# Retention followed by a tanh-shrink feed-forward on one core: down product interleaved with the up product, factored polynomial, retention and weight conversion moved into block 0

## The chip, the core and the metric

The kernel runs on one core of one Trainium2 chip. A core has five engines that run beside each other and wait for each other by semaphores: TensorE (PE in the profile; its weight loads are PEld), VectorE (DVE), ScalarE (ACT), GpSimd (POOL) and SyncE (SP, which here issues all DMAs). The metric is device microseconds of one execution, the median of several; lower is better.

## The reference, cut to what matters

```
# first part: q, k, v are [4, 8, 768, 64] float32
for t in range(S):                                   # S = 768 positions
    state = gamma[h] * state + outer(k[t], v[t])     # per batch and head, 64x64
    y[t]  = scale * (q[t] @ state)
x = y.transpose(0, 2, 1, 3).reshape(3072, 512)
# second part: w_in [512, 2048], w_out [2048, 512], both float64
h   = x @ w_in
out = (h - tanh(h)) @ w_out
```

[...] For small h the difference h - tanh(h) is made by a polynomial in u = h*h, for u of at least 0.5 by subtracting.

## The kernel before

**Tiling.** The 3072 rows of x are 24 chunks of 128 positions, and 6 blocks of 4 chunks (512 rows). Each of the 32 weight pieces is [128, 512]. `chunk(ci)` makes one chunk of the first part: POOL scales q and k by decays (L167), PE transposes both (L173, into the tile tp), ACT copies them out of PSUM (L176), PE makes k'v for the running state (L184), DVE updates the state in four half-height operations (L195, L197), PE makes the scores (L203), DVE masks them (L208, two operations), PE adds the part of the earlier state (L214) and of the scores (L218) into y, and ACT copies y into xT (L221).

**The second part.** For block n and column tile m (16 of each block), `up(n, m)` makes h = x w_in as four matmuls of 512 columns (L229; each shows as two records in the trace, so 768 records in all). ACT copies h to SBUF (L233) and makes u = h*h (L234) and tanh (L235). POOL makes the mask u >= 0.5 (L236) and h - tanh(h) (L237). DVE runs a Horner chain of five operations (L240), a sixth that multiplies by h (L244), and a predicated copy (L246) that ends the tile g. `down(n, j)` multiplies g of all 16 column tiles by w_out, 16 matmuls into one accumulator in PSUM (L252, two records each), ACT copies it out (L255), and SP writes it (L256).

**Weights.** `weights` loads one piece and converts it: one ACT operation (L129), six DVE operations (L124, L126, L128, L132, L134, L135) and three POOL operations (L130, L131, L137).

**What sets the order.** The kernel is written in a plain order: eight chunks with the 16 pieces of w_in between them, then block by block all 16 `up`, with one chunk of two blocks ahead after every fourth, and then the four `down`. A scheduler reorders it: each engine's queue is the scheduler's. Tiles of PSUM are held by tag: h has two banks, o one, tp two, s two, y one. Each engine then runs its own queue strictly in order.

```
    for n in range(NB):
        for m in range(NM):
            up(n, m)
            ...
        for j in range(BLK):
            down(n, j)
```

Of the kernel before, what the change touches and what calls it, by code (L numbers as in the profile page):

```python
# [10 lines left out]
I32 = mybir.dt.int32  # L11
# [9 lines left out]
G = [  # L21
    0.3333333270366726,
    -0.1333324237000098,
    0.05394671405955269,
    -0.02168005900277128,
    0.00808936284945116,
    -0.002039037268817698,
]
# [3 lines left out]
def kernel(  # L32
# [34 lines left out]
    stage = ctx.enter_context(tc.tile_pool(name="stage", bufs=4))  # L67
    inp = ctx.enter_context(tc.tile_pool(name="inp", bufs=3))
    mid = ctx.enter_context(tc.tile_pool(name="mid", bufs=2))
    xp = ctx.enter_context(tc.tile_pool(name="xp", bufs=3))  # L70
    tmp = ctx.enter_context(tc.tile_pool(name="tmp", bufs=2))
    gp = ctx.enter_context(tc.tile_pool(name="gp", bufs=20))
    op = ctx.enter_context(tc.tile_pool(name="op", bufs=2))
    ps = ctx.enter_context(tc.tile_pool(name="ps", bufs=1, space=bass.MemoryType.PSUM))

    def bank(tag, bufs):
        return ps.tile([P, TB], F32, tag=tag, name=tag, bufs=bufs)
# [5 lines left out]
    tab = cst.tile([P, tables.shape[1]], F32, name="tab")  # L83
    nc.sync.dma_start(out=tab, in_=tables)
    gq = tab[:, 0:H]
    gk = tab[:, H : 2 * H]
    gchunk = tab[:, 2 * H : 2 * H + NP]
    ident = tab[:, 2 * H + NP : 2 * H + NP + P]
    causal = tab[:, 2 * H + NP + P : 2 * H + NP + 2 * P]

    states = []
    for i in range(2):
        t = cst.tile([P, NP, P], F32, name=f"state{i}")
        nc.vector.memset(t, 0.0)
        states.append(t)

# [1 line left out]
    w1 = wts.tile([P, NC, DF], F32, name="w1")  # L98
    w2 = wts.tile([P, NM, DM], F32, name="w2")

    def work(tag, dtype=F32):
        return tmp.tile([P, TB], dtype, tag=tag, name=tag)

    def weights(dst, src):
# [10 lines left out]
        raw = stage.tile([P, 2 * TB], U32, tag="raw", name="raw")  # L115
        nc.sync.dma_start(out=raw, in_=src.bitcast(U32))
        raw = raw.rearrange("p (n two) -> p two n", two=2)
        lo, hi = raw[:, 0], raw[:, 1]
        head = work("h", U32)
        power = work("u", U32)  # L120
        low = work("th")
        e = work("a", U32)
        fits = work("m")
        nc.vector.tensor_scalar(head, hi, 3, 0x3FFFFFF8, op0=ALU.logical_shift_left,  # L124
# [4 lines left out]
        nc.scalar.activation(low, lo, AF.Copy, scale=2.0 ** -52)  # L129
        nc.gpsimd.tensor_tensor(low, low, power.bitcast(F32), op=ALU.mult)  # L130
        nc.gpsimd.tensor_tensor(dst, low, head.bitcast(F32), op=ALU.add)  # L131
        nc.vector.tensor_scalar(e, hi, 20, 0x7FF, op0=ALU.logical_shift_right,  # L132
                                op1=ALU.bitwise_and)
        nc.vector.tensor_scalar(fits, e, 1023.0 + 128.0, 3.0e38, op0=ALU.is_ge, op1=ALU.mult)  # L134
        nc.vector.scalar_tensor_tensor(fits, in0=e, scalar=1023.0 - 126.0, in1=fits,  # L135
                                       op0=ALU.is_ge, op1=ALU.max)
        nc.gpsimd.tensor_tensor(dst, dst, fits, op=ALU.mult)  # L137

    def load_w_in(fb):
        for c in range(NC):  # L140
            weights(w1[:, c, ts(fb, TB)], w_in[ts(c, P), ts(fb, TB)])

    def load_w_out(m):
        weights(w2[:, m], w_out[ts(m, P)])

# [1 line left out]
    loaded = {}  # L147
    xT = {}
    state = [None]
    n_state = [0]  # L150

    def load_chunk(ci):
        b, j = divmod(ci, CPB)
        loaded[ci] = []
        for nm, src in (("q", q), ("k", k), ("v", v)):
# [4 lines left out]
    def chunk(ci):  # L160
# [4 lines left out]
        qh, kh, vb = loaded.pop(ci)  # L165
        for t, g in ((qh, gq), (kh, gk)):
            nc.gpsimd.tensor_tensor(t, t, g[:, :, None].to_broadcast([P, H, D]), op=ALU.mult)  # L167

        turned = []
        for t in (qh, kh):  # L170
            tp = bank("tp", 2)
            for p in range(NP):
                nc.tensor.transpose(tp[:, ts(p, P)],  # L173
                                    t[:, ds(2 * p, 2)].rearrange("p h d -> p (h d)"), ident)
            s = mid.tile([P, NP, P], F32, tag=f"T{len(turned)}", name=f"T{len(turned)}_{ci}")
            nc.scalar.copy(out=s, in_=quarters(tp))  # L176
            turned.append(s)
        qT, kT = turned

        before = state[0] if j else None  # L180
        if j < CPB - 1:
            kv = bank("tp", 2)
            for p in range(NP):
                nc.tensor.matmul(kv[:, ts(p, P)],  # L184
                                 kh[:, ds(2 * p, 2)].rearrange("p h d -> p (h d)"),
                                 vb[:, ds(2 * p, 2)].rearrange("p h d -> p (h d)"),
                                 start=True, stop=True)
            after = states[n_state[0] % 2]
            n_state[0] += 1
            for i in range(2):  # L190
                r = ds(D * i, D)
                new, g = after[r, :, r], gchunk[r, :, None].to_broadcast([D, NP, D])
                src = quarters(kv)[r, :, r]
                if before is not None:
                    nc.vector.tensor_tensor(new, src, before[r, :, r], op=ALU.add)  # L195
                    src = new
                nc.vector.tensor_tensor(new, src, g, op=ALU.mult)  # L197
            state[0] = after

        sp = [bank("s", 2) for _ in range(2)]  # L200
        for h in range(H):
            r = ds(D * (h % 2), D)
            nc.tensor.matmul(sp[h % 2][:, ts(h // 2, P)], kT[r, h // 2], qT[r, h // 2],  # L203
                             start=True, stop=True)
# [129 lines left out]
```

## Time and profile before

| | |
|---|---|
| median of 3 runs | 1131.55 us (1128.22 to 1133.97) |
| span of the profiled execution (first to last instruction) | 1128.5 us; no time of its own is listed beside it |
| mean granted TensorE clock | 0.895 |
| PE busy | 885.3 us, 78% of the span |
| DVE busy | 794.2 us, 70% |
| POOL busy | 564.4 us, 50% |
| ACT busy | 242.9 us, 22% |
| moved by DMA | 42.63 MB, mean 38 GB/s |

The page cuts the span into 40 slices and gives each engine's busy share as a digit. Its chain is the work that ended last, followed back from the end; shares are of the span. Matmul records are pipelined: a record's duration is longer than the time from its start to the next one's start, so a rate is read from starts. A granted clock of 1.00 is 2.4 GHz and 0.50 is 1.2 GHz.

### The profile page before, as it was taken

Reading aid. Unit: us, or ns where it says so; the run is one execution under the profiler, and the core shown is the slowest. Engines: PE = TensorE matmul, PEld = TensorE weight load, DVE = VectorE, ACT = ScalarE, POOL = GpSimd, SP = SyncE. Lnnn points to the kernel's source line nnn. Section 1 sums busy time; section 2 is a strip of 40 time slices with the busy share of each in tenths; the row PEclk is TensorE's granted clock in tenths of the full one; section 3 lists DMA queues with packets and bytes.
Section 4 is the critical chain, followed back from the end, with each engine's and each line's share of the span. In section 5 each row is a group of like instructions: output and inputs, shape, how many; then the busy total and the mean of one; then the engine's idle time right before and its main releaser. Section 6 shows DMA issues by size and latency. Waiting matters only on the chain.

```text
span 1128.5 us, 8323 instructions
## 1 busy us (share of the span) xinstructions
PE 885.3 (78%) x2816; PEld 433.4 (38%) x2816; DVE 794.2 (70%) x986; ACT 242.9 (22%) x417; POOL 564.4 (50%) x340
## 2 busy tenths in 40 slices
PE   5336755657699987899777798888997788997788
PEld 4224521324244443444434343544443333433333
DVE  5999999899992599503999404999108996279910
ACT  2111221222231233102333002332003231132200
POOL 4877787766771357303555203565007872156800
PEclk9566967878899998899898899898999999998989
DMA  9344441211010001100111100000000000000000
GB/s 227 104 121 94 150 116 43 66 56 38 9 38 19 19 19 29 29 19 26 31 34 24 28 19 19 19 1 1 18 10 10 1 0 10 19 10 0 0 19 19
DMA packets 83131, 42.63 MB, mean 38 GB/s; under 512 B 75792, under 2 KB 75920, under 8 KB 83088
## 3 DMA queue, kind: packets, MB, share of 16 engines
q1 hardware_dynamic: 83088, 42.09, 14.2%
q8 instruction: 22, 0.36, 0.1%
q14 instruction: 21, 0.17, 0.0%
HBM read 35.79 MB, written 6.29 MB: 37 GB/s over the span
## 4 chain that ended last, share of the span: by engine, by line
DVE 52%; PE 32%; issue 10%; POOL 3%; ACT 2%; DMA 0%; ACTq 0%; SPq 0%; POOLq 0%; DVEq 0%
PE o L252 25%; DVE a L240 24%; DVE g L246 6%; DVE g L244 6%; PE h L229 4%; DVE a L132 3%; DVE h L124 3%; DVE a L208 2%; DVE m L134 2%; DVE state L197 2%; PE y L218 2%; POOL th L237 1%; DVE m L135 1%; DVE h L126 1%; DVE state L195 1%
## 5 line engine op out<-in xcount | busy, mean ns | idle before, releaser
L229 PE MATMUL h<-xT,w 128*128 128x512 f32 x768 | 395.5, 663 | 95.6 <-ACT h L233 95.6
L236 POOL TENSOR_SCALAR m<-u 128x512 int32<-128x512 f32 x96 | 218.9, 2281 | 416.2 <-ACT u L234 413.1
L252 PE MATMUL o<-w,g 128*128 128x512 f32 x768 | 349.8, 606 | 12.1 <-DVE g L246 9.9
L240 DVE SCALAR_TENSOR_TENSOR a<-a,u 128x512 f32<-128x512 f32 x384 | 344.4, 915 | 2.2
L229 PEld LDWEIGHTS h<-xT,w 128*128 128x128 f32 x768 | 156.4, 212 | 295.8 <-issue 177.1
L240 DVE SCALAR_TENSOR_TENSOR a<-u 128x512 f32<-128x512 f32 x96 | 85.8, 896 | 246.6 <-ACT u L234 246.5
L252 PEld LDWEIGHTS o<-w,g 128*128 128x128 f32 x768 | 144.6, 193 | 198.5 <-issue 162.7
L237 POOL TENSOR_TENSOR th<-h,th 128x512 f32<-128x512 f32 x96 | 143.8, 1498 | 20.4 <-ACT th L235 20.4
L233 ACT COPY h<-h 128x512 f32<-128x512 f32 x96 | 56.2, 585 | 364.9 <-DVE g L244 169.0
L246 DVE COPY_PREDICATED g<-m,th 128x512 f32<-128x512 int32 x96 | 86.6, 904 | 15.6 <-POOL th L237 14.8
L244 DVE SCALAR_TENSOR_TENSOR g<-a,h 128x512 f32<-128x512 f32 x96 | 85.2, 889 | 0.5
L218 PE MATMUL y<-a,v 128*64 128x128 f32 x384 | 45.4, 334 | 46.4 <-DVE a L208 46.3
L130 POOL TENSOR_TENSOR th<-th,u 128x512 f32<-128x512 f32 x32 | 53.0, 1656 | 45.9 <-DVE u L128 43.9
L255 ACT COPY o<-o 128x512 f32<-128x512 f32 x24 | 14.0, 585 | 281.2 <-PE o L252 281.1
L218 PEld LDWEIGHTS y<-a,v 128*64 128x64 f32 x384 | 31.9, 167 | 77.6 <-DVE a L208 66.6
L235 ACT ACTIVATE th<-h 128x512 f32<-128x512 f32 x96 | 60.0, 625 | 7.0 <-DVE g L246 7.0
L234 ACT ACTIVATE u<-h 128x512 f32<-128x512 f32 x96 | 60.6, 632 | 2.7
L173 PE MATMUL tp<-tab,q 128*128 128x128 f32 x96 | 17.1, 308 | 53.6 <-DVE state L195 38.1
L137 POOL TENSOR_TENSOR w<-w,m 128x512 f32<-128x512 f32 x32 | 49.0, 1531 | 11.6 <-DVE m L135 10.4
L203 PE MATMUL s<-T,T 64*128 64x128 f32 x384 | 38.6, 322 | 11.5 <-ACT T L176 11.4
L131 POOL TENSOR_TENSOR w<-th,h 128x512 f32<-128x512 f32 x32 | 42.6, 1333 | 2.3
L132 DVE TENSOR_SCALAR a<-raw 128x512 uint32<-128x512 uint32 x32 | 40.6, 1268 | 0.0
(28 smaller groups left out, 508.7 us busy)
## 6 DMA issues: line engine op xcount, KB each, us to landing
raw<-in_moe_w_in_dram SPq DMA_DIRECT2D x16, 512.0 KB, 4.2
raw<-in_moe_w_out_dram SPq DMA_DIRECT2D x16, 512.0 KB, 3.8
q<-in_q_dram SPq DMA_DIRECT2D x24, 256.0 KB, 3.4
k<-in_k_dram SPq DMA_DIRECT2D x24, 256.0 KB, 3.8
v<-in_v_dram SPq DMA_DIRECT2D x24, 256.0 KB, 3.1
out_dram<-o SPq DMA_DIRECT2D x24, 256.0 KB, 2.0
tab<-in_tables_dram SPq DMA_DIRECT2D x1, 138.0 KB, 2.3
```

Of the source, the lines that this page charges most:

```text
L132: nc.vector.tensor_scalar(e, hi, 20, 0x7FF, op0=ALU.logical_shift_right, op1=ALU.bitwise_and)
L218: nc.tensor.matmul(yT[ds(D * i, D), ts(p, P)], vb[:, h], a[i][:, p], start=(before is None and p == 0), stop=True, skip_group_check=True)
L229: nc.tensor.matmul(hp, w1[:, c, ts(m, P)], xT[n][:, c], start=(c == 0), stop=(c == NC - 1))
L233: nc.scalar.copy(out=h, in_=hp)
L234: nc.scalar.activation(u, h, AF.Square)
L235: nc.scalar.activation(th, h, AF.Tanh)
L236: nc.gpsimd.tensor_scalar(large, u, U_SMALL, None, op0=ALU.is_ge)
L237: nc.gpsimd.tensor_tensor(th, h, th, op=ALU.subtract)
L240: nc.vector.scalar_tensor_tensor(a, in0=prev, scalar=c / G[-1], in1=u, op0=ALU.add, op1=ALU.mult)
L244: nc.vector.scalar_tensor_tensor(g, in0=a, scalar=G[-1], in1=h, op0=ALU.mult, op1=ALU.mult)
L246: nc.vector.copy_predicated(g, large, th)
L252: nc.tensor.matmul(o_p, gT[n, m][:, ts(j, P)], w2[:, m], start=(m == 0), stop=(m == NM - 1))
```

## The change

**Order.** The automatic scheduler is off (`manual_schedule`): each engine's queue is in the order of the code. The first part's work of a chunk is cut into `load_chunk`, `scale_chunk`, `turn` (transposes and copies), `scores` (with the masks) and `outputs`. Eight chunks and eight weight pieces (four of w_in, four of w_out) come ahead of the second part; the other 16 chunks and 24 pieces stand inside block 0, one chunk with each column tile and two pieces with each of the first twelve. From block 1 on only `up`, `shrink` and `down` are left. The down product of a column tile follows the up product two tiles later (LAG), into four accumulators at once.

**Shrink.** ACT makes u, tanh, two squares (q0, q1) and the mask (a Relu of u - 0.5); all five read PSUM or u, and no copy of h is made. DVE makes two factors and their product (L270, L273, L274, L277), h - tanh(h) in place in PSUM (L272), and the predicated copy (L278), whose source is in PSUM. POOL has no part in it.

**Retention.** Decays are by position in the whole sequence, so the state needs no scaling; DVE updates it in one operation of 512 columns (L235 or L237). The state's part of y is eight products of 64 x 64 by 128 columns (L226) in place of four of 128 x 128.

**Conversion.** Two ACT operations (L145, L146), four DVE operations (L147, L149, L151, L153) and two POOL operations (L154, L155) for one piece.

**PSUM and SBUF.** All eight banks are one pool. The raw pieces have two buffers (four before), g five (twenty before), xT six.

```
+    AHEAD = 8
+    LAG = 2
...
+    ps = ctx.enter_context(tc.tile_pool(name="ps", bufs=8, space=bass.MemoryType.PSUM))
+    ctx.enter_context(tc.manual_schedule())
...
+    def convert(i):
...
+        nc.scalar.activation(low, lo, AF.Copy, scale=2.0 ** -52)
+        nc.scalar.activation(head.bitcast(F32), hi.bitcast(F32), AF.Abs)
+        nc.vector.tensor_scalar(head.bitcast(F32), head.bitcast(F32), HI_MIN, HI_MAX,
+                                op0=ALU.max, op1=ALU.min)
+        nc.vector.tensor_scalar(head, head, 3, 0x3FFFFFF8, op0=ALU.logical_shift_left,
                                 op1=ALU.bitwise_and)
         nc.vector.scalar_tensor_tensor(head, in0=hi, scalar=0xC0000000, in1=head,
                                        op0=ALU.bitwise_and, op1=ALU.bitwise_or)
         nc.vector.tensor_scalar(power, head, 0xFF800000, None, op0=ALU.bitwise_and)
         nc.gpsimd.tensor_tensor(low, low, power.bitcast(F32), op=ALU.mult)
         nc.gpsimd.tensor_tensor(dst, low, head.bitcast(F32), op=ALU.add)
...
+    def shrink(n, m):
+        hp = hps.pop((n, m))
+        u, th, q0, q1, large, t = (work(x) for x in ("u", "th", "q0", "q1", "large", "t"))
+        nc.scalar.activation(u, hp, AF.Square)
+        nc.scalar.activation(th, hp, AF.Tanh)
+        nc.scalar.activation(q0, u, AF.Square, bias=bias0)
+        nc.scalar.activation(q1, u, AF.Square, bias=bias1, scale=math.sqrt(A))
+        nc.scalar.activation(large, u, AF.Relu, bias=bias_m)
+        nc.vector.scalar_tensor_tensor(t, in0=u, scalar=R, in1=hp, op0=ALU.subtract,
+                                       op1=ALU.mult, reverse0=True)
+        nc.vector.tensor_tensor(hp, hp, th, op=ALU.subtract)
+        nc.vector.scalar_tensor_tensor(q0, in0=q0, scalar=C0, in1=t, op0=ALU.add, op1=ALU.mult)
+        nc.vector.scalar_tensor_tensor(q1, in0=q1, scalar=A * C1, in1=q0, op0=ALU.add,
+                                       op1=ALU.mult)
...
+        nc.vector.tensor_tensor(g, q1, u, op=ALU.mult)
+        nc.vector.copy_predicated(g, large.bitcast(I32), hp)
...
+    for ci in range(AHEAD):
+        scores(ci)
+        load_chunk(ci + 2)
+        scale_chunk(ci + 1)
+        if ci + 1 < AHEAD:
+            turn(ci + 1)
+        outputs(ci)
+        convert(ci)
+        load_weights(ci + 2)
...
     for n in range(NB):
         for m in range(NM):
+            ci = AHEAD + n * NM + m
+            if ci < NCH:
+                load_chunk(ci + 2)
+                convert(w)
+                load_weights(w + 2)
+                turn(ci)
             up(n, m)
+            if ci < NCH:
+                scores(ci)
+                scale_chunk(ci + 1)
+            shrink(n, m)
+            waiting.append((n, m))
+            downs(LAG)
+            if ci < NCH:
+                outputs(ci)
+                convert(w + 1)
+                load_weights(w + 3)
+                w += 2
```

The three places on which the prediction's terms rest follow. Names are tile, block and column tile (or chunk), and a buffer number. First PE from block 1 on; before, at the end of block 1 (o is an accumulator, g_1_14 the tile of column tile 14, h the next block's first product):

```order
L252 MATMUL o_2377<-w2_92,g_1_12_2246 128x512
L252 MATMUL o_2377<-w2_92,g_1_13_2269 128x512
L252 MATMUL o_2377<-w2_92,g_1_14_2292 128x512
L252 MATMUL o_2377<-w2_92,g_1_15_2315 128x512
L229 MATMUL h_2457<-xT_2_1064,w1_91 128x512
L252 MATMUL o_2397<-w2_92,g_1_0_1798 128x512
L252 MATMUL o_2397<-w2_92,g_1_1_1821 128x512
L252 MATMUL o_2397<-w2_92,g_1_2_1844 128x512
```

and now, inside block 1:

```order
L258 MATMUL h_1_5_2496<-xT_1_448,w1_89 128x512 x4
L284 MATMUL o_1_0_2434<-w2_90,g_1_3_2462 128x512
L284 MATMUL o_1_1_2436<-w2_90,g_1_3_2462 128x512
L284 MATMUL o_1_2_2438<-w2_90,g_1_3_2462 128x512
L284 MATMUL o_1_3_2440<-w2_90,g_1_3_2462 128x512
L258 MATMUL h_1_6_2523<-xT_1_448,w1_89 128x512 x4
L284 MATMUL o_1_0_2434<-w2_90,g_1_4_2489 128x512
L284 MATMUL o_1_1_2436<-w2_90,g_1_4_2489 128x512
L284 MATMUL o_1_2_2438<-w2_90,g_1_4_2489 128x512
L284 MATMUL o_1_3_2440<-w2_90,g_1_4_2489 128x512
```

The 16 matmuls into one accumulator have become four into four accumulators, for one g, behind the four of an up product two tiles later.

Second, POOL in the part ahead of the second part; before (q and k are chunk 3's, th, w1 and m belong to conversions):

```order
L130 TENSOR_TENSOR th_180<-th_180,u_179 128x512
L131 TENSOR_TENSOR w1_91<-th_180,h_178 128x512
L137 TENSOR_TENSOR w1_91<-w1_91,m_182 128x512
L167 TENSOR_TENSOR q_3_227<-q_3_227,tab_85 128x512
L130 TENSOR_TENSOR th_197<-th_197,u_196 128x512
L167 TENSOR_TENSOR k_3_229<-k_3_229,tab_85 128x512
L131 TENSOR_TENSOR w1_91<-th_197,h_195 128x512
L137 TENSOR_TENSOR w1_91<-w1_91,m_199 128x512
```

and now (low, w1 are conversions of pieces 2 and 3):

```order
L180 TENSOR_TENSOR k_3_204<-k_3_204,tab_87 128x512
L180 TENSOR_TENSOR q_3_206<-q_3_206,tab_87 128x512
L154 TENSOR_TENSOR low_2_327<-low_2_327,power_2_326 128x512
L155 TENSOR_TENSOR w1_89<-low_2_327,head_2_325 128x512
L180 TENSOR_TENSOR k_4_278<-k_4_278,tab_87 128x512
L180 TENSOR_TENSOR q_4_280<-q_4_280,tab_87 128x512
L154 TENSOR_TENSOR low_3_401<-low_3_401,power_3_400 128x512
L155 TENSOR_TENSOR w1_89<-low_3_401,head_3_399 128x512
```

The scaling of chunk ci + 2 now stands right behind the two operations of conversion ci, and a conversion has two operations in place of three.

Third, DVE in block 0; before (a, h, u, m of lines 124 to 135 belong to a conversion):

```order
L240 SCALAR_TENSOR_TENSOR a_946<-u_944 128x512
L124 TENSOR_SCALAR h_963<-raw_961 128x512
L240 SCALAR_TENSOR_TENSOR a_946<-a_946,u_944 128x512
L126 SCALAR_TENSOR_TENSOR h_963<-raw_961,h_963 128x512
L240 SCALAR_TENSOR_TENSOR a_946<-a_946,u_944 128x512
L128 TENSOR_SCALAR u_964<-h_963 128x512
L240 SCALAR_TENSOR_TENSOR a_946<-a_946,u_944 128x512
```

and now, one iteration (masks of chunk 16, shrink of column tile 8, state, then conversions 25 and 26 start):

```order
L209 TENSOR_TENSOR a0_16_1623<-s0_16_1613,tab_87 128x512
L209 TENSOR_TENSOR a1_16_1625<-s1_16_1614,tab_87 128x512
L270 SCALAR_TENSOR_TENSOR t_1634<-u_1629,h_0_8_1608 128x512
L272 TENSOR_TENSOR h_0_8_1608<-h_0_8_1608,th_1630 128x512
L273 SCALAR_TENSOR_TENSOR q0_1631<-q0_1631,t_1634 128x512
L274 SCALAR_TENSOR_TENSOR q1_1632<-q1_1632,q0_1631 128x512
L277 TENSOR_TENSOR g_0_8_1644<-q1_1632,u_1629 128x512
L278 COPY_PREDICATED g_0_8_1644<-large_1633,h_0_8_1608 128x512
L237 TENSOR_TENSOR state_16_1666<-kv_16_1661,state_15_1551 128x512
L147 TENSOR_SCALAR head_25_1677<-head_25_1677 128x512
L149 TENSOR_SCALAR head_25_1677<-head_25_1677 128x512
L151 SCALAR_TENSOR_TENSOR head_25_1677<-raw_25_1573,head_25_1677 128x512
L153 TENSOR_SCALAR power_25_1678<-head_25_1677 128x512
```

The conversions no longer alternate with the polynomial: the two masks, six operations of a shrink and the state's update stand together, and two whole conversions follow them. The shown rows end after the first.

## Rows read from the trace of the kernel before

**Rows 1.** The page: the span in 40 slices; the chain by engine.

```profile
span 1128.5 us, 8323 instructions
...
PE   5336755657699987899777798888997788997788
...
DVE  5999999899992599503999404999108996279910
...
DVE 52%; PE 32%; issue 10%; POOL 3%; ACT 2%; DMA 0%; ACTq 0%; SPq 0%; POOLq 0%; DVEq 0%
```

**Rows 2.** Groups by line: shapes xcount | busy us, mean ns | idle before.

```profile
L240 DVE SCALAR_TENSOR_TENSOR a<-a,u 128x512 f32<-128x512 f32 x384 | 344.4, 915 | 2.2
...
L208 DVE TENSOR_TENSOR a<-s,tab 128x512 f32<-128x512 f32 x48 | 31.7, 685 | 3.3 <-PE s L203 2.6
...
L129 ACT ACTIVATE th<-raw 128x512 f32<-128x512 uint32 x32 | 21.6, 676 | 74.1 <-POOL w L131 54.9 <-DVE g L246 17.6 <-DMA raw<-in_moe_w_in_dram 1.2
...
L221 ACT COPY xT<-y 128x512 f32<-128x512 f32 x24 | 14.0, 583 | 109.7 <-PE y L218 109.7
```

**Rows 3.** Timeline of PE, warm: start, us, operation, xrecords.

```profile
616.67 0.60 PE L173 MATMUL tp<-tab,q 128*128 128x128 f32 x4
617.11 0.60 PE L173 MATMUL tp<-tab,k 128*128 128x128 f32 x4
617.54 1.02 PE L252 MATMUL o<-w,g 128*128 128x512 f32 x2
618.40 1.05 PE L184 MATMUL tp<-v,k 128*128 128x128 f32 x8
619.39 1.16 PE L203 MATMUL s<-T,T 64*128 64x128 f32 x16
620.48 1.16 PE L214 MATMUL y<-T,state 128*128 128x128 f32 x8
```

**Rows 4.** Windows: length, busy us of PE, PEld, DVE, ACT, POOL; granted clock.

```profile
28.00:44.00 16.00, 8.21 (x38) 6.56 (x39) 16.00 (x16) 3.57 (x6) 13.56 (x10) 0.50 0.44 113
815.00:830.00 15.00, 15.00 (x36) 6.57 (x35) 0.00 (x0) 0.58 (x1) 0.00 (x0) 1.00 0.05 17
```

**Rows 5.** Timeline, first chunks.

```profile
4.69 1.04 POOL L167 TENSOR_TENSOR q<-q,tab 128x512 f32<-128x512 f32 x1 [4.27 <-DMA q<-in_q_dram]
...
6.88 1.11 PE L173 MATMUL tp<-tab,k 128*128 128x128 f32 x4
...
11.64 0.66 PE L173 MATMUL tp<-tab,q 128*128 128x128 f32 x4
...
13.44 1.09 PE L218 MATMUL y<-a,v 128*64 128x128 f32 x14
...
40.10 1.97 PE L218 MATMUL y<-a,v 128*64 128x128 f32 x14 [0.99 <-DVE a L208]
```

**Rows 6.** Timeline, conversions: DVE beside an idle and beside a busy POOL.

```profile
17.85 0.42 DVE L124 TENSOR_SCALAR h<-raw 128x512 uint32<-128x512 uint32 x1
...
18.52 0.68 DVE L126 SCALAR_TENSOR_TENSOR h<-raw,h 128x512 uint32<-128x512 uint32 x1
...
25.77 1.58 POOL L130 TENSOR_TENSOR th<-th,u 128x512 f32<-128x512 f32 x1 [1.37 <-DVE u L128]
26.15 1.48 DVE L124 TENSOR_SCALAR h<-raw 128x512 uint32<-128x512 uint32 x1
27.43 1.32 POOL L131 TENSOR_TENSOR w<-th,h 128x512 f32<-128x512 f32 x1
```

**Rows 7.** Timeline, second part: polynomial on DVE, an activation on ACT.

```profile
542.29 1.75 DVE L244 SCALAR_TENSOR_TENSOR g<-a,h 128x512 f32<-128x512 f32 x1
...
553.04 2.14 DVE L240 SCALAR_TENSOR_TENSOR a<-a,u 128x512 f32<-128x512 f32 x3
...
560.37 0.63 ACT L235 ACTIVATE th<-h 128x512 f32<-128x512 f32 x1
```

**Rows 8.** Timeline: the last copy out of PSUM.

```profile
1124.97 0.58 ACT L255 COPY o<-o 128x512 f32<-128x512 f32 x1 [14.13 <-PE o L252]
```

More of the change, by code (lines that the diff above doesn't have):

```diff
@@ L84, with columns, weight_ends, load_weights @@
     nc.sync.dma_start(out=tab, in_=tables)
[L85 to L95, printed above, removed]
+    at = [0]
+    def columns(n):
+        at[0] += n
+        return tab[:, at[0] - n : at[0]]
+    gq = columns(CPB * H)
+    gk = columns(CPB * H)
+    ident = columns(P)
+    causal = columns(P)
+    bias0, bias1, bias_m = columns(1), columns(1), columns(1)
     w1 = wts.tile([P, NC, DF], F32, name="w1")
     w2 = wts.tile([P, NM, DM], F32, name="w2")
-    def work(tag, dtype=F32):
-        return tmp.tile([P, TB], dtype, tag=tag, name=tag)
-    def weights(dst, src):
+    raws = {}
+    def weight_ends(i):
+        f, r = divmod(i, 2 * NC)
+        if r < NC:
+            return w1[:, r, ts(f, TB)], w_in[ts(r, P), ts(f, TB)]
+        m = NC * f + r - NC
+        return w2[:, m], w_out[ts(m, P)]
+    NW = 2 * NM
+    def load_weights(i):
+        if i >= NW:
+            return
+        dst, src = weight_ends(i)
         if src.dtype == F32:
@@ L178, in chunk @@
[L178 to L186, printed above, removed]
-                                 start=True, stop=True)
[L188 to L197, printed above, removed]
-            state[0] = after
@@ L200, in chunk @@
[L200 to L204, printed above, removed]
-        a = []
-        for i in range(2):
-            a.append(mid.tile([P, NP, P], F32, tag=f"a{i}", name=f"a{i}_{ci}"))
-            nc.vector.tensor_tensor(a[i], quarters(sp[i]),
-                                    causal[:, None, :].to_broadcast([P, NP, P]), op=ALU.mult)
@@ L211, in chunk @@
-        yT = bank("y", 1)
-        if before is not None:
-            for p in range(NP):
-                nc.tensor.matmul(yT[:, ts(p, P)], before[:, p], qT[:, p], start=(p == 0),
-                                 stop=False, skip_group_check=True)
+        kh, _, vb = loaded.pop(ci)
+        _, qT = turned.pop(ci)
+        a = masked.pop(ci)
+        before = state[0] if j else None
+        yT = bank(f"y_{ci}")
+        if before is not None:
+            for h in range(H):
+                r = ds(D * (h % 2), D)
+                nc.tensor.matmul(yT[r, ts(h // 2, P)], before[r, h // 2, r], qT[r, h // 2],
+                                 start=(h // 2 == 0), stop=False, skip_group_check=True)
@@ new lines, in outputs @@
+        if j < CPB - 1:
+            kv = bank(f"kv_{ci}")
+            for p in range(NP):
+                nc.tensor.matmul(kv[:, ts(p, P)], pair(kh, p), pair(vb, p),
+                                 start=True, stop=True)
+            after = mid.tile([P, NP, P], F32, tag="state", name=f"state_{ci}")
+            if before is None:
+                nc.vector.tensor_copy(after, quarters(kv))
+            else:
+                nc.vector.tensor_tensor(after, quarters(kv), before, op=ALU.add)
+            state[0] = after
@@ L224, with work @@
     gT = {}
+    o_p = {}
+    def work(tag, dtype=F32):
+        return tmp.tile([P, TB], dtype, tag=tag, name=tag)
+    hps = {}
     def up(n, m):
-        hp = bank("h", 2)
+        hp = bank(f"h_{n}_{m}")
         for c in range(NC):
@@ L259, in next_chunk, with down @@
-    def next_chunk(ci):
-        if ci + 2 < NCH:
-            load_chunk(ci + 2)
-        if ci < NCH:
-            chunk(ci)
+    def down(n, m, j):
+        if m == 0:
+            o_p[n, j] = bank(f"o_{n}_{j}")
+        nc.tensor.matmul(o_p[n, j], gT[n, m][:, ts(j, P)], w2[:, m], start=(m == 0),
+                         stop=(m == NM - 1))
+        if m == NM - 1:
+            o = op.tile([P, DM], F32, tag="o", name=f"o_{n}_{j}")
+            if j % 2:
+                nc.vector.tensor_copy(o, o_p[n, j])
+            else:
+                nc.scalar.copy(out=o, in_=o_p[n, j])
+            nc.sync.dma_start(out=out[ds(n * TB + j * P, P)], in_=o)
@@ L287, in _tables @@
+    for j in range(BLK):
+        for n, m in waiting:
+            down(n, m, j)
+def _tables(H, D, S=768):
     import numpy as np
```

167 lines of the change are left out of this document (78 added, 89 removed).

## The prediction

> **What bounds the kernel now.** I read the page's slices and chain first. In the slices PE and DVE take turns: from the middle of the span on, DVE stands at 9 for some slices while PE is at 7 or 8, and then DVE falls as low as 0 while PE is at 8 or 9 [rows 1]. The chain gives DVE 52% of the span and PE 32% [rows 1]. So a block is two phases one behind the other: 16 up products at the pace of DVE's polynomial, then four down products in which DVE has nothing to do. Then I looked for the pace of PE when nothing holds it. In a down phase it is busy all the time at a granted clock of 1.00, its upper level of 2.4 GHz [rows 4], and two records of 512 columns take 0.86 us from start to start, 0.43 each [rows 3]. A column tile has four up and four down products, 16 records: 6.88 us. For 96 tiles that is 660 us, far under the span. Last I looked at why DVE is slow where it is slow. Beside an idle POOL a one-input operation takes 0.42 us and a two-input one 0.68; beside a POOL product the same one-input operation takes 1.48 and ends only after the product [rows 6], and a two-input one 1.75 [rows 7]. The mean of the polynomial's operation is 0.915 [rows 2]. The mask from PSUM, which has one input in SBUF, stays at 0.685 on average [rows 2], so it doesn't wait for POOL.
>
> **The change, part by part.** I follow the new order in four stretches. Within a stretch I look for the loop that comes back to its own start; its length is the period.
>
> *Blocks 1 to 5.* PE's queue is four up products of tile m, four down products of tile m-2, and nothing else. PE needs 6.88 us a tile. DVE has six operations: two with an operand in PSUM at 0.685, and four in a dependent chain at 0.73 each (three such in 2.14 us with the last at 0.68 [rows 7]), 4.3 us. ACT has five at 0.63 [rows 7], 3.2 us. POOL has no instruction left, so nothing lengthens DVE's. g of tile m is ready some 5.5 us after its up product (two activations, 1.3, then DVE's 4.3), and its down product is due only after three more groups of 3.44 us on PE beyond the one that runs, 13.8 us. Hence PE doesn't wait; the two engines that are moved off the path hide beneath it, and would set the pace only above 6.88 us a tile. Waits for a bank stand only at column tiles 3 and 4 of a block, on copies of the last accumulators that have a whole group of 3.44 us to be made in. From the start of block 1 there are 80 tiles of up and 82 of down (two are behind): (80 + 82) x 8 = 1296 records x 0.43 = 557 us.
>
> *The last tile.* Its g is due 4.3 us after its up product (one group and one product) and ready after 5.5: 1.2 us of wait. From the last copy's start at 1124.97 to the span's end 3.5 us pass now [rows 1, 8], with the way from PE to the copy 3.8. Together 5.
>
> *Block 0, first twelve tiles.* Here PE has 6.88 us and a chunk: transposes 0.87, scores 1.09, k'v 0.99, the state's part as k'v 0.99, and y as the scores 1.09 [rows 3], 5.0 in all, so 11.9. The state's eight half-size products aren't in the trace; their bounds are half of that 0.99 and twice it. DVE has two conversions, two masks, the shrink and the state. PE's next up product waits for the state's update, since that releases its bank; so the loop runs through DVE. From the end of one update: the first conversion takes 3 x 0.42 + 0.68 + 3 hand-overs of 0.05 = 2.1. Now POOL starts on it, 1.66 from start to start and then 1.32 [rows 6], and DVE's second conversion runs into both products: two of its operations wait, and it ends at 6.6 in place of 4.2. The masks end at 7.9, the two operations on PSUM at 9.15. POOL meanwhile, from 6.7, does the second conversion's two products (3.0) and the scaling of two tiles (1.04 alone [rows 5], with DVE beside it 1.3), and is done at 12.3. Three two-input operations of the shrink get one slot behind each of POOL's last three: 12.7. The predicated copy makes it 13.4, the state 14.1. PE is done with k'v at 10 and does not set the loop. The period is 14.1 us, x 12 = 169. Bounds: if POOL and DVE never met, PE's 11.9 would hold (26 us less in all). If every DVE operation kept out of POOL's way, it would be DVE's 10.4 (two conversions 4.2, five operations on PSUM 3.3, four in the chain 2.9) and POOL's 2 x 3.0 + 2 x 1.3 = 8.6 in a row, 19.0 (59 us more).
>
> Two operations of the shrink, t and h - tanh(h), have one input in SBUF and one in PSUM. The row nearest to them is the mask's 0.685, the other end is the polynomial's 0.915 [rows 2]; I take the mask's. The Trainium skill (SBUF — State Buffer, Who interferes with whom) says that a DVE instruction with at most one SBUF input, outside its two-port modes, doesn't contend with GpSimd, and that with two it does; by it the period stays at 14.1. Were both held like the row of 1.48, it would be 15.7 and the total 19 us more.
>
> *Block 0, last four tiles.* No conversion is left: DVE's masks, shrink and state take 6.3, and PE's 11.9 hold. 4 x 11.9 = 48.
>
> *The eight chunks ahead.* This part gets a loop that the old order doesn't have. On PE, the transposes of chunk ci+2 stand ahead of the y of chunk ci+1; on POOL their scaling stands behind conversion ci; that one waits on ACT behind the copy of y of chunk ci. So from y to the next y everything stands in a row: copy and two activations 0.583 + 2 x 0.676 = 1.94 [rows 2], DVE's four operations 2.1, POOL's two products 3.0, two scalings 2.1, the last transposes 1.1, state, k'v and y, with 0.5 for five hand-overs between engines. PE waits over 6 us in it; in a stretch of the present kernel where PE is busy half the time its granted clock is 0.50, the lower level of 1.2 GHz [rows 4], and y takes 1.97 in place of 1.09 [rows 5]. All cold it is 16.5 us, all warm (transposes 0.6) 13.3. In the first chunk transposes are cold at 6.88 and warm at 11.64 [rows 5], so I take y alone as warm: 15.6. The first y ends at 14.5 [rows 5], six loops follow, 93.6, and from there to the end of chunk 8's transposes 10.6 (the loop without its last three terms and with 0.4 for hand-overs): the first up product starts at 118.7. DMA isn't in it: by the shapes a loop loads 1.25 MB, and each load is sent a loop ahead.
>
> *Sum.* 118.7 + 169 + 48 + 557 + 5 = 898 us of span. The runs' median is 3.05 above the profiled span; with it 901 us, 20% less than before.
>
> **The rivals.**
>
> *POOL and DVE exclude each other altogether in block 0.* For it: in the conversions of the present kernel nearly every one-input operation shows 1.48. Against it: the mask doesn't. 901 + 59 = 960.
>
> *The short loops.* PE stays warm in the first part and the two engines seldom meet: 901 - 6 x 2.3 - 26 = 861. Against it speaks the 0.50 [rows 4].
>
> *Slower: DVE sets blocks 1 to 5.* The tile in PSUM is read and written in place by DVE, and no row shows that, nor a predicated copy out of PSUM. If the six operations took as long as the longest row, 1.75 [rows 7], a tile would take 10.5 us: 901 + 80 x 3.62 = 1191. It turns slower than before above 1.63 us an operation, (1132 - 901) / 80 = 2.9 us more a tile. That row belongs to a busy POOL, and POOL's queue is empty there.
>
> *The overlap doesn't come about,* since something in PE's queue waits for g after all. A wait of 2.9 us a tile would bring the old time back; no instruction of PE's queue in those blocks waits on a tile younger than two.
>
> **How the numbers follow.** Forecast 0.70, POOL and DVE excluding each other 0.14, short loops 0.11, DVE sets the pace 0.04, no overlap 0.01. The predicted time is the first's, 901. The range goes from the short loops, 862, to 955, just under the first rival, which leaves out its upper half, the slower case and little else. A measurement of this kernel can tell 0.5%, some 6 us, from no change. Faster by more than that: 0.95; within: 0.01; slower: 0.04.
>
> **What would show it.** Blocks 1 to 5 right: PE without idle time at clock 1.00, 6.9 us from one h to the next, DVE near 60% and POOL at nothing. Block 0 right: some 14 us between state updates, DVE's one-input operations near 1.5 beside POOL. The first part right: 15 to 16 us from y to y, clock near 0.5, the first h near 119. Wrong: an h later than 140, idle time of PE that DVE ends in blocks 1 to 5, or any DVE operation over 1.1 us there.

## The result, and the profile after

The changed kernel takes 884.88 us (median of 5 runs, 880.28 to 886.51), where the kernel before takes 1131.55 (1128.22 to 1133.97): a ratio of 0.7818, with a 95% interval of 0.7794 to 0.7841. The prediction was 901 us, 862 to 955. The profiled execution took 880.28 us, with a span of 878.5; the median lies 6.4 us above that span. Of the four runs of the kernel with phases and two banks further down, one took 1132.91 us at a granted clock of 0.744, a slower state, and is left out of its median.

The page of the changed kernel, beside [rows 1]: the span, the slices of PE and DVE, the granted clock, and the chain's shares by engine.

```profile
span 878.5 us, 8488 instructions
...
PE   4644789898889999999999999999999999999997
...
DVE  2233499989996546555566555655556655566554
...
PEclk9778689999999999999999999999999999999999
...
PE 77%; DVE 13%; POOL 3%; issue 2%; ACT 2%; DMA 1%; SPq 0%; DVEq 0%; POOLq 0%; ACTq 0%
```

The turns of PE and DVE are gone. From the sixteenth slice to the last but one PE stands at 9 at full clock, DVE at 5 or 6 beside it. The chain, 52% DVE and 32% PE before, is 77% PE. DVE stands at 8 or 9 only in slices 6 to 12, which lie in the first twelve tiles of block 0.

The same by the prediction's stretches (ahead of the first h; twelve tiles of block 0; its last four; from block 1 to the last up product; the rest). The columns are busy time and instructions of each engine, the granted clock, the DMA share and rate.

```profile
core 0: us, PE busy (x) PEld busy (x) DVE busy (x) ACT busy (x) POOL busy (x), PEclk, DMA share, GB/s
0.00:105.17 105.17, 55.47 (x481) 45.17 (x481) 29.19 (x54) 25.39 (x44) 36.06 (x36) 0.79 0.55 121
105.17:268.95 163.78, 146.75 (x897) 85.60 (x897) 153.27 (x200) 78.92 (x142) 95.72 (x72) 0.95 0.55 134
268.95:316.82 47.87, 47.55 (x307) 27.49 (x305) 26.80 (x39) 18.56 (x33) 9.54 (x8) 1.00 0.16 31
316.82:862.40 545.58, 545.58 (x1274) 241.60 (x1273) 322.10 (x484) 235.92 (x406) 0.00 (x0) 1.00 0.03 10
862.40:878.50 16.10, 11.15 (x26) 4.47 (x24) 5.38 (x8) 4.08 (x7) 0.00 (x0) 1.00 0.17 65
```

In the fourth row PE is busy for all of its 545.58 us. One h follows the other by 6.87 us there, with a down group between them. Of the h that starts at 502.32, DVE's six operations run from 507.07 to 511.39, 4.32 us:

```profile
502.32 3.60 PE L258 MATMUL h<-xT,w 128*128 128x512 f32 x8
...
507.07 0.69 DVE L270 SCALAR_TENSOR_TENSOR t<-u,h 128x512 f32<-128x512 f32 x1 [2.55 <-ACT th L266]
...
509.19 3.60 PE L258 MATMUL h<-xT,w 128*128 128x512 f32 x8
...
510.66 0.73 DVE L278 COPY_PREDICATED g<-large,h 128x512 f32<-128x512 int32 x1
```

### The profile page after: what moved, and what is told of

The parts are those of the page before. It is cut to its first block, busy times and chain, and to the rows that moved or that the text cites. A ratio compares the mean times of both kernels' runs of the same rounds, so it can differ in the third digit from the quotient of the medians.

```text
span 878.5 us, 8488 instructions
## 1 busy us (share of the span) xinstructions
PE 806.5 (92%) x2976; PEld 404.3 (46%) x2976; DVE 536.7 (61%) x784; ACT 362.9 (41%) x629; POOL 141.3 (16%) x116
## 4 chain that ended last, share of the span: by engine, by line
PE 77%; DVE 13%; POOL 3%; issue 2%; ACT 2%; DMA 1%; SPq 0%; DVEq 0%; POOLq 0%; ACTq 0%
PE h L258 35%; PE o L284 34%; DVE head L151 2%; DVE head L149 2%; PE y L226 2%; PE y L241 2%; DVE q L274 1%; DVE g L277 1%; PE qTp L194 1%; PE kv L231 1%; DVE a L209 1%; DVE q L273 1%; PE kTp L194 1%; POOL low L154 1%; PE s L204 1%
## 5 line engine op out<-in xcount | busy, mean ns | idle before, releaser
L258 PE MATMUL h<-xT,w 128*128 128x512 f32 x768 | 351.3, 601 | 1.5 <-DVE g L278 1.5
L270 DVE SCALAR_TENSOR_TENSOR t<-u,h 128x512 f32<-128x512 f32 x96 | 65.7, 684 | 190.4 <-ACT th L266 190.4
L274 DVE SCALAR_TENSOR_TENSOR q<-q,q 128x512 f32<-128x512 f32 x96 | 74.9, 780 | 10.4 <-DVE q L273 0.5
L277 DVE TENSOR_TENSOR g<-q,u 128x512 f32<-128x512 f32 x96 | 73.8, 768 | 8.0 <-DVE q L274 0.5
L278 DVE COPY_PREDICATED g<-large,h 128x512 f32<-128x512 int32 x96 | 70.3, 732 | 9.9
L273 DVE SCALAR_TENSOR_TENSOR q<-q,t 128x512 f32<-128x512 f32 x96 | 70.5, 734 | 0.0
L267 ACT ACTIVATE q<-u,tab 128x512 f32<-128x512 f32 x96 | 69.3, 722 | 0.0
L268 ACT ACTIVATE q<-u,tab 128x512 f32<-128x512 f32 x96 | 68.9, 718 | 0.0
L269 ACT ACTIVATE large<-u,tab 128x512 f32<-128x512 f32 x96 | 68.7, 716 | 0.0
L272 DVE TENSOR_TENSOR h<-h,th 128x512 f32<-128x512 f32 x96 | 66.5, 692 | 0.0
L194 PE MATMUL kTp<-tab,k 128*128 128x128 f32 x96 | 20.3, 348 | 47.9 <-POOL k L180 47.9
L154 POOL TENSOR_TENSOR low<-low,power 128x512 f32<-128x512 f32 x32 | 41.2, 1287 | 130.3 <-DVE power L153 115.6
L244 ACT COPY xT<-y 128x512 f32<-128x512 f32 x24 | 14.1, 586 | 93.9 <-PE y L241 93.9
L155 POOL TENSOR_TENSOR w<-low,head 128x512 f32<-128x512 f32 x32 | 41.4, 1292 | 2.5
```

Source lines behind the costliest of these rows:

```text
L258: nc.tensor.matmul(hp, w1[:, c, ts(m, P)], xT[n][:, c], start=(c == 0), stop=(c == NC - 1))
L267: nc.scalar.activation(q0, u, AF.Square, bias=bias0)
L268: nc.scalar.activation(q1, u, AF.Square, bias=bias1, scale=math.sqrt(A))
L269: nc.scalar.activation(large, u, AF.Relu, bias=bias_m)
L270: nc.vector.scalar_tensor_tensor(t, in0=u, scalar=R, in1=hp, op0=ALU.subtract, op1=ALU.mult, reverse0=True)
L272: nc.vector.tensor_tensor(hp, hp, th, op=ALU.subtract)
```

## Experiments on the interleave

The theory: blocks 1 to 5 gain because ACT's and DVE's work of a tile lies wholly beside PE's 6.88 us, and two tiles of lag cover the way from h to g. The rival: the shorter polynomial and the empty POOL bring the gain, whatever the order.

**Phases again.** In blocks 1 to 5 all 16 up products come first, then all down products, with two banks for h. (The pools of block 0 are closed behind it to make room for 20 tiles g. The down products still go tile by tile into four accumulators.)

```
+            hp = late["ps"].tile([P, TB], F32, tag="h", name=f"h_{n}_{m}", bufs=2)
...
-            downs(LAG)
+            if n == 0:
+                downs(LAG)
...
+        downs(0)
```

> The changed kernel, but in blocks 1 to 5 all 16 up products come first and all 64 down products after them, with two banks for h as in the kernel before; block 0 is unchanged. Theory (the interleave is what hides DVE's polynomial): the up phase runs at DVE's 4.3 us a tile. 3.44 + 1.2 + 14 x 4.3 + 3.44 = 68.3 us, then 55 us of down products with DVE idle, 123.3 us a block in place of 110: 5 x 13.3 = 66 more, 885 + 66 = 951 us (940 to 965), PE idle about 13 us a block behind DVE's predicated copy. Rival (the gain comes from the shorter polynomial and the empty POOL, the order is beside the point): 885 to 890 us.

Measured: 970.9 us (970.06 to 972.88), 86 more than the changed kernel. The rival falls, since the order is worth 86 us with the shrink and POOL's queue as they are. But the theory's price was 66 and its range ended at 965, so its up phase at DVE's own pace was wrong. The same kernel was run once more for its rows.

> The kernel of the run with phases and two banks for h once more, for the rows of its trace. Theory (a loop over two tiles sets its up phase: predicated copy, up product 3.44, two activations 1.2, DVE's chain 4.3 and hand-overs 0.2, 9.1 in all): the start of every second up product 9.1 us behind the last but one, DVE waiting some 0.3 us in each tile for ACT's tanh, and 126 to 128 us from one block's first up product to the next one's; 970 us. Rival (DVE alone, 4.3 us a tile): DVE without idle time in an up phase, and the excess over 110 us a block lies in the down phase.

It took 971.09 us. PE's rows in that kernel, of an up phase and of the first two up products of two blocks:

```profile
340.39 3.70 PE L263 MATMUL h<-xT,w 128*128 128x512 f32 x8 [2.12 <-DVE g L283]
...
349.54 3.70 PE L263 MATMUL h<-xT,w 128*128 128x512 f32 x8 [1.34 <-DVE g L283]
...
584.38 7.03 PE L263 MATMUL h<-xT,w 128*128 128x512 f32 x16
...
710.92 7.03 PE L263 MATMUL h<-xT,w 128*128 128x512 f32 x16
```

Every second up product starts 9.15 us after the last but one (340.39 to 349.54): with two banks the loop runs from the predicated copy through the next up product but one, two activations and DVE's chain back to it. So a tile costs 4.57 us, not DVE's 4.3. From one block's first up product to the next one's (584.38 to 710.92) it is 126.5 us in place of 110. Five times 16.5 makes 83 of the 86; the sum had taken 123.3, DVE's own pace.

**Phases with four banks for h.**

```
-            hp = late["ps"].tile([P, TB], F32, tag="h", name=f"h_{n}_{m}", bufs=2)
+            hp = late["ps"].tile([P, TB], F32, tag="h", name=f"h_{n}_{m}", bufs=4)
```

> As the run with phases (970 us), but with four banks for h in blocks 1 to 5 in place of two. Theory (with two banks a loop predicated copy, up product, two activations, DVE's chain, predicated copy closes over two tiles: 3.44 + 1.2 + 4.3 + 0.2 = 9.1, 4.6 us a tile, and PE may be only two tiles ahead of DVE when the down products begin): with four banks DVE alone sets 4.3 us, and the last up product starts behind the predicated copy of tile 11: 3.44 + 1.2 + 12 x 4.3 + 3.44 = 59.7, with 55 of down products 115 us a block in place of 127; 5 x 12 = 60 less, 910 us (900 to 922). Rival (the phases cost for another reason, the four down products in a row or the order itself): 960 us or more.

Measured: 903.98 us, only 19 above the interleaved order. Its rows of PE:

```profile
444.90 41.63 PE L263 MATMUL h<-xT,w 128*128 128x512 f32 x96
...
502.84 55.10 PE L292 MATMUL o<-w,g 128*128 128x512 f32 x128
557.77 2.74 PE L263 MATMUL h<-xT,w 128*128 128x512 f32 x6
```

A block is 112.9 us (444.90 to 557.77). DVE, once it has started, goes at 4.12 us a tile without a wait, while PE may run four tiles ahead of it and starts the down products at 502.84, 12.9 us ahead of the end of DVE's last tile. So 67 of the 86 us that the phases cost came from the few banks that PE had to run ahead in, and not from their order as such. The interleaved order needs less room: the h that starts at 502.32 is done with at 511.39, ahead of the start of the next but one (6.87 on from 509.19), so no more than two are alive at once. It was not run with only two banks for h.

**The old polynomial in the new order** (blocks 1 to 5).

```
-            shrink(n, m)
+            (horner if n else shrink)(n, m)
```

Here `horner` is the kernel before's L233 to L246.

> The changed kernel, but in blocks 1 to 5 a tile's polynomial is that of the kernel before: ACT copies h and makes u and tanh, POOL the mask and h - tanh(h), DVE five Horner steps, a product and the predicated copy. Theory (what hides beside PE's 6.88 us a tile costs nothing): DVE's seven operations take 5 x 0.90 + 0.98 + 0.78 = 6.3 us and 0.3 for their spacing, by the durations of the kernel before in its up phases, 6.6 us, under 6.88; so 885 us, plus about 3 for the last tile's longer wait: 888 (883 to 900). Rival (the factored polynomial is needed): DVE sets the pace, at 7.5 us a tile or more, 885 + 80 x 0.6 = 935 us or more, and PE's idle time in blocks 1 to 5 ends on DVE.

Measured: 886.97 us, 2 more than the changed kernel, whose own runs span 6 us. In the trace a block is as long as before, 109.9 us from its first h to the next one's. Only at the last tile PE waits 3.58 us in place of 1.22, and its records behind that wait take 7.97 us in place of 6.28. Two of DVE's rows of a tile, and that wait:

```profile
503.98 0.69 DVE L300 SCALAR_TENSOR_TENSOR q<-u 128x512 f32<-128x512 f32 x1 [0.39 <-ACT u L294]
...
509.71 0.74 DVE L306 COPY_PREDICATED g<-large,th 128x512 f32<-128x512 int32 x1
...
874.43 7.97 PE L312 MATMUL o<-w,g 128*128 128x512 f32 x14 [3.58 <-DVE g L306]
```

DVE has 0.39 us left in 6.87. The factored polynomial and the empty POOL thus bring next to nothing in blocks 1 to 5 once the products are interleaved. In the phase order they are worth more: in the last up phase of the kernel before there are 13 steps from one copy of h to the next between the two rows below, 74.70 / 13 = 5.75 us each, against 4.57 with the new shrink and the same two banks. The 1.2 us a tile are an estimate, since the two kernels differ in more than the shrink there.

```profile
992.33 0.58 ACT L233 COPY h<-h 128x512 f32<-128x512 f32 x1 [2.89 <-PE h L229]
...
1067.03 0.58 ACT L233 COPY h<-h 128x512 f32<-128x512 f32 x1 [3.91 <-DVE g L244]
```

The kernel with phases, two banks and the new shrink is 161 us faster than the kernel before. How these 161 divide among the shrink, the empty POOL and the new place of the first part, no run separates.

**Four more DVE operations a tile** (blocks 1 to 5).

```
+        for _ in range(4 if n else 0):
+            nc.vector.tensor_tensor(q1, q1, q1, op=ALU.max)
```

> The changed kernel with four more DVE operations in each tile of blocks 1 to 5, in the chain (the larger of q1 and q1, which changes no value). Theory (DVE is hidden up to PE's 6.88 us a tile and sets the pace above it): DVE takes 4.3 + 4 x 0.79 = 7.5 us, so 0.6 us a tile more, 80 x 0.6 = 48 and 3 at the last tile: 935 us (922 to 945), and PE's idle time ends on DVE. Rival (each DVE operation lies on the path, or none does): 885 + 80 x 3.2 = 1140, or 888.

Measured: 924.84 us, 40 more. From one predicated copy to the next DVE takes 7.10 us there, 0.22 above PE's pace, and PE waits at the turn of each block:

```profile
458.71 2.07 PE L286 MATMUL o<-w,g 128*128 128x512 f32 x2 [4.25 <-DVE g L280]
```

Per block DVE needs 16 x 7.10 and the two copies of o, 0.7 each, with 2.2 us of wait between them for the output's transfer: 117.2, against 110 for PE. The block measures 116.8 (458.71 to the next such wait at 575.49). The first of the five blocks still uses up the room of the lag and takes 111.1; the last one ends with waits of 3.39 and 5.20 in place of 1.22. From the first h of block 1 to the end it is 601.2 us in place of 561.7, the 40 measured. So DVE sets the pace above PE's 6.88 us and costs nothing below it: the turning point that the prediction's slower rival used.

**No lag, and one tile of lag.**

```
-    LAG = 2
+    LAG = 0
```

> The changed kernel with LAG = 0: a tile's down products stand right behind its own up product on PE. Theory (the two tiles of lag hide the latency from h to g, some 5.5 us): PE waits for g in every tile, 3.44 + 1.2 + 4.3 + 0.2 + 3.44 = 12.6 us in place of 6.88, 80 x 5.7 = 456 more in blocks 1 to 5 and 50 to 90 more in block 0: 1400 us (1350 to 1440), slower than the kernel before. Rival (the interleave itself is enough, without the lag): under 1000 us.

Measured: 1663.82 us (one run), slower than the kernel before. The mechanism is the expected one, the price was missed by 260. A tile of PE and the next up group, then the stretches of two down groups and of the up group between them, where the last number but two is the granted clock:

```profile
799.69 3.60 PE L258 MATMUL h<-xT,w 128*128 128x512 f32 x8
808.80 5.21 PE L284 MATMUL o<-w,g 128*128 128x512 f32 x8 [5.52 <-DVE g L278]
813.85 3.60 PE L258 MATMUL h<-xT,w 128*128 128x512 f32 x8
```

```profile
808.80:813.85 5.05, 5.05 (x8) 2.28 (x9) 0.00 (x0) 0.00 (x0) 0.00 (x0) 0.70 0.00 0
813.85:817.40 3.55, 3.55 (x9) 1.33 (x7) 0.00 (x0) 0.00 (x0) 0.00 (x0) 1.00 0.00 0
822.96:829.46 6.50, 6.50 (x9) 2.72 (x10) 0.00 (x0) 0.00 (x0) 0.00 (x0) 0.54 0.00 0
```

The wait is 5.52 us, as the prediction had the way from h to g (5.5). But in the down group behind it the granted clock is 0.70 and 0.54, and the group takes 5.05 and 6.50 us in place of 3.44; the up group that follows has 1.00 again. A tile is 14.2 or 15.6 us (799.69 to 813.85, and from there to 829.46), not 12.6. A wait of PE is paid a second time in clock here. From the first h of block 1 to the end it is 1188 us in place of 562, so 627 more where 456 were expected. The rest of the miss lies in block 0: 364 us in place of 212, 153 more where 50 to 90 were expected, and in each of its last four tiles PE waits 9.5 us for g.

With LAG = 1:

> The changed kernel with LAG = 1: a tile's down products stand behind the next tile's up product. Theory (g is ready 5.5 us after its own up product, by the 5.52 us that PE waited with LAG = 0): it is due after one group of down and one of up products, 6.88 us, so PE waits in blocks 1 to 5 still nowhere; only the last tile's wait grows a little: 885 us (882 to 890). Rival (two tiles of lag are needed, since the engines' hand-overs add up): 885 + 80 x 1 or more.

Measured: 891.8 us, 7 more, 2 beyond the expected range. Within a block PE waits nowhere, as expected. At the five turns it waits 1.19, 0.64, 0.55, 1.18 and 0.86 us, since DVE's copies of o stand ahead of the chain there and one of them waits for the output's transfer:

```profile
338.37 0.69 DVE L289 COPY o<-o 128x512 f32<-128x512 f32 x1 [4.07 <-DMA out_dram<-o]
```

These 4.4 us and 0.9 more at the last tile are 5.3 of the 7. Another 2.0 are clock: behind the last tile's wait of 2.08 us the granted clock is 0.69, and the eight records there take 5.40 us in place of 3.44.

```profile
882.08 5.40 PE L284 MATMUL o<-w,g 128*128 128x512 f32 x8 [2.08 <-DVE g L278]
```

```profile
882.00:887.50 5.50, 5.40 (x8) 2.02 (x8) 0.72 (x2) 1.17 (x2) 0.00 (x0) 0.69 0.24 95
```

So in blocks 1 to 5 the second tile of lag is needed for the turns and the end alone.

## Experiments on the first part and on block 0

**Conversion ahead of the outputs.** The prediction's first part is a loop from y to the next y in which everything stands in a row. Here the conversion (of a weight piece's 64-bit words to float32) is put ahead of y's copy in every queue.

```
+        convert(ci)
+        load_weights(ci + 2)
         outputs(ci)
-        convert(ci)
-        load_weights(ci + 2)
```

> The changed kernel, but in the part ahead of block 0 the conversion of piece ci stands ahead of the outputs of chunk ci in every queue, not behind them. Theory (the part ahead is set by a loop from y through the copy, two activations, DVE's four conversion steps, POOL's two products and two scalings to the next transposes): the loop is cut, POOL's products run beside PE's work, and a chunk takes 7 to 8.5 us in place of 13.7; six chunks save 5 to 6.5 us each, 30 to 40 us: 845 to 855 us, the first h near 70. Rival (loads or PE's own work set the 13.7 us): within 5 us of 885.

Measured: 856.63 us, 28 less, and 2 beyond the expected range. The loop is real, but what the edit left is longer than expected: y now follows y by 9.6 to 10.1 us in the full loops behind the first one (11.1), and the first h stands at 82.2, since POOL's products still stand ahead of the scaling that the next transposes need, and start only behind the activations that follow ACT's copies of the last ones.

**Scaling one chunk earlier as well**, ahead of the products in POOL's queue (in block 0 too).

```
         scores(ci)
-        load_chunk(ci + 2)
-        scale_chunk(ci + 1)
+        scale_chunk(ci + 2)
...
         outputs(ci)
+        load_chunk(ci + 3)
```

> The changed kernel with the conversion ahead of the outputs, as in the run that gave 857, and with POOL's scaling one chunk earlier, ahead of the conversion's two products; the chunk's load stands behind the outputs. Theory (what is left of the loop in the first part goes from POOL's products through the scaling, the transposes, ACT's copies and two activations and DVE's four steps back to the products, 9.7 us): it is cut too, and a chunk takes PE's own work and the meeting of DVE and POOL, 6 to 7 us; seven chunks save some 3 us each: the first h near 62, 836 us (828 to 846). Rival (the loads take that time): 852 us or more.

Measured: 839.6 us (838.99 to 843.38), 45 less than the changed kernel: a ratio to the kernel before of 0.7422, with an interval of 0.7404 to 0.7441. This is the best version. Two of its rows y, two loops of 6.3 us apart, and its first part:

```profile
23.15 1.09 PE L241 MATMUL y<-a,v 128*64 128x128 f32 x16
...
35.76 1.09 PE L241 MATMUL y<-a,v 128*64 128x128 f32 x16
```

```profile
0.00:63.21 63.21, 47.35 (x481) 38.58 (x482) 38.21 (x54) 24.69 (x42) 40.06 (x37) 0.97 0.92 203
```

Nearly the same instructions as in the first stretch of the changed kernel take 63.21 us in place of 105.17, the clock is 0.97 in place of 0.79, and DMA moves 203 GB/s, so that the loads were not what set 13.7 us. They are near it now: DMA is busy 0.92 of the stretch, and between 16 and 60 us POOL waits 10.0 us in all for a chunk's k to land.

**No scaling in block 0.** POOL's two scalings are left out for its chunks, and the tables are ones.

```
                 scores(ci)
-                scale_chunk(ci + 1)
```

> The changed kernel without POOL's two scalings of q and k for the chunks of block 0 (left out of the computation; the decay tables are all ones so that values stay small). Theory (block 0's 13.65 us a tile is set by DVE, whose two-input operations wait behind POOL's): the shrink's third, fourth and fifth operations go from 1.01, 1.35 and 1.42 to 0.7 to 0.8 each, 1.5 us less a tile, and the period is 12.1 to 12.4: 12 x 1.4 = 17 us less, 868 us (864 to 874). Rival (PE's queue sets the period): 883 to 887 us, period still 13.6.

Measured: 871.42 us, 13.5 less. The first twelve tiles take 150.3 us (first h at 110.14, the thirteenth tile's at 260.40), 12.52 a tile in place of 13.65: the whole gain is theirs, and PE had room for it. DVE's chain with the scalings (the first three rows, of the changed kernel) and without:

```profile
209.30 1.01 DVE L273 SCALAR_TENSOR_TENSOR q<-q,t 128x512 f32<-128x512 f32 x1
...
210.41 1.35 DVE L274 SCALAR_TENSOR_TENSOR q<-q,q 128x512 f32<-128x512 f32 x1
...
211.79 1.42 DVE L277 TENSOR_TENSOR g<-q,u 128x512 f32<-128x512 f32 x1
```

```profile
205.71 1.00 DVE L273 SCALAR_TENSOR_TENSOR q<-q,t 128x512 f32<-128x512 f32 x1
206.82 0.69 DVE L274 SCALAR_TENSOR_TENSOR q<-q,q 128x512 f32<-128x512 f32 x1
207.55 0.69 DVE L277 TENSOR_TENSOR g<-q,u 128x512 f32<-128x512 f32 x1
```

Two operations get their 0.69 back; the first keeps its 1.00, where the theory had all three fall, since the conversion's last product is still ahead of it. So the wait of DVE's two-input operations for POOL is a price of block 0 that is on the path, some 1.1 us a tile for the scalings alone.

## Why the prediction was right, and where its sizes were off

The span was summed to 898 us and is 878.5. Of the 19 us between them 13.5 lie in the first part and 5.2 in the first twelve tiles of block 0; the rest of the sum is met within 0.5. The step from span to median was 3.3 too small, so the time is off by 16.

**Blocks 1 to 5 and the last tile: right.** 557 + 5 us from the start of block 1 were forecast, 561.7 measured (316.82 to 878.5). The last tile's wait was 1.2 in the sum and is 1.22 in the trace. DVE is at 322.10 of 545.58, 59%. The longest DVE operation there is the predicated copy, 0.73 on average and at most 0.74. h - tanh(h), read and written in place in PSUM, takes 0.69, no more than the mask took before. So the slower rival is gone.

**Block 0: right, 5 us too long.** 14.1 us a tile were forecast, 13.65 measured, 163.8 us in place of 169; the last four tiles took 47.9 where 48 stood. The working can be followed in the tile whose state begins at 200.29 and the next at 213.93:

```profile
203.17 1.31 POOL L154 TENSOR_TENSOR low<-low,power 128x512 f32<-128x512 f32 x1 [4.15 <-DVE power L153]
203.40 1.37 DVE L149 TENSOR_SCALAR head<-head 128x512 uint32<-128x512 uint32 x1
...
204.56 1.33 POOL L155 TENSOR_TENSOR w<-low,head 128x512 f32<-128x512 f32 x1
...
208.10 0.68 DVE L270 SCALAR_TENSOR_TENSOR t<-u,h 128x512 f32<-128x512 f32 x1
208.49 1.27 POOL L155 TENSOR_TENSOR w<-low,head 128x512 f32<-128x512 f32 x1
208.70 0.69 DVE L272 TENSOR_TENSOR h<-h,th 128x512 f32<-128x512 f32 x1
...
209.71 1.49 POOL L180 TENSOR_TENSOR k<-k,tab 128x512 f32<-128x512 f32 x1
...
211.17 1.49 POOL L180 TENSOR_TENSOR q<-q,tab 128x512 f32<-128x512 f32 x1
```

DVE's second conversion does run into POOL's first two products (1.37 in place of 0.43), and h - tanh(h), with one input in PSUM, stays at 0.69 in the middle of a product. Three sizes were off, and they cancel in part. DVE's second conversion ends 6.0 us after the state and not 6.6: POOL's products follow each other by 1.39 us where the sum took 1.66 [rows 6], and the terms that the sum prints (2.1 + 1.66 + 1.32, then 0.68 and 0.42) make 6.2. POOL's second pair of products takes 2.58 us (207.13 to 209.71) and not 3.0. Against that its scalings take 1.47 each beside DVE and not 1.3. So POOL is done at 11.7 in place of 12.3, and the next state at 13.6 in place of 14.1.

That the loop runs through DVE is right, but not because the up product waits for the state's update: DVE itself waits for others only 3.4 of the 163.8 us, so its own queue is the loop, and PE waits mostly at the transposes of q, for the bank that the predicated copy releases (10.3 us in six waits).

The rule of the Trainium skill (SBUF — State Buffer, Who interferes with whom), that a DVE instruction with at most one input in SBUF keeps clear of GpSimd outside the two-port modes, agrees with the 0.68 of t and the 0.69 of h - tanh(h) here.

**The first part: the loop was right, its length was not.** The first h was forecast at 118.7 and came at 105.17. From the first y at 13.70 to the seventh at 93.61 it is 79.9 us, where the sum had six loops of 15.6. Four loops take 13.7, and by the prediction's own signs this part is a miss: not 15 to 16 us from y to y, a mean clock of 0.79 and not near 0.5, the first h not near 119. The first and the seventh y, and then rows of a loop:

```profile
13.70 1.09 PE L241 MATMUL y<-a,v 128*64 128x128 f32 x16
...
93.61 1.41 PE L241 MATMUL y<-a,v 128*64 128x128 f32 x16
```

```profile
65.64 1.73 PE L226 MATMUL y<-qT,state 64*64 64x128 f32 x16
...
67.30 1.16 PE L231 MATMUL kv<-v,k 128*128 128x128 f32 x8
...
73.61 1.26 POOL L154 TENSOR_TENSOR low<-low,power 128x512 f32<-128x512 f32 x1 [9.07 <-DVE power L153]
...
77.27 1.12 PE L194 MATMUL kTp<-tab,k 128*128 128x128 f32 x4 [6.69 <-POOL k L180]
```

Three terms were too large. POOL's two products beside an idle DVE take 1.26 each, 2.6 with the gap, in place of 3.0. The copy and two activations overlap: 1.7 in place of 1.94. And the clock came back earlier than taken. It is 0.50 in the transposes (63.60 to 65.64), which is the lower level, 0.59 in the state's part (65.64 to 67.30) and 1.00 in k'v (67.30 to 68.39). These two take 1.7 and 1.1 us, 2.8 together, where 15.6 leaves 3.8 for them. By these three the loop is 15.6 - 0.4 - 0.25 - 1.0 = 13.95, and the last 0.3 is in shorter hand-overs. (With twice 0.99 for each of the two, the terms that the prediction lists add up to 16.7 all cold and 15.8 with y warm, not to 16.5 and 15.6.) The two remaining loops take 12.6 us, since chunk 5 makes no k'v and chunk 6 has no earlier state; the sum counted them as full.

**From the span to the median**, 3.05 us were added and it is 6.4. The profiled run was the quickest of the five. Seven other kernels here have the same first part, and in a trace of each the first h stands at 108.3 to 110.8 in place of 105.17. The second chunk's k reaches POOL at 10.2 to 11.4 there in place of 9.82, the first y starts at 15.2 to 16.4 in place of 13.70, and the next loop takes 14.1 to 15.6 in place of 13.64. So a later load of the first chunks, which nothing hides, is 0.4 to 1.5 us of it. With LAG = 1, for one, the second chunk's k'v also takes 1.92 us and not 1.06. Why it does is open, and none of this was tried by itself.

Of the rivals, the short loops were half right: their first part of 105 us came about, though the clock did fall in it (0.79), but their 11.9 us a tile in block 0 did not. So the 105 us came by another way than this rival's. That POOL and DVE exclude each other altogether did not come about either. The case made for it was a misreading: of the 128 one-input operations in the conversions of the kernel before, 49 take over 1.4 us, and 62 stay under 0.5.

## What to carry to other kernels

Where two engines take turns in phases, give the waiting one work that is due later than the other's latency, and count that latency in groups of its own work. Once the slower engine's work fits beside the bound one's, shortening it further brings nothing, and the next gain is where instructions of all engines still stand in one row: another order of the first part's steps brought 45 us here, the factored polynomial 2 in blocks 1 to 5, which is less than the runs differ by. The same overlap could be had in the phase order to within 19 us with two more banks.

## What the runs showed of the hardware

A DVE operation of 128x512 that reads the result of the one ahead starts 0.72 to 0.80 us after it (206.82 and 207.55 in the rows without scaling), an independent one 0.60 (208.10 and 208.70 in the rows of block 0), though all of them show a duration of some 0.69. So six operations take 4.3 us alone in their tile, and 4.12 where tiles follow each other without a wait.

A wait of 5.5 us cost TensorE 1.6 to 3.1 us more in the 3.44 us of work behind it (granted clock 0.70 and 0.54, where 1.00 is 2.4 GHz and 0.50 is 1.2), which no sum had. Behind the wait of 2.08 us with LAG = 1 it cost 2.0 (0.69); behind the wait of 1.22 us in the changed kernel the granted clock stayed at 1.00.
